# ELU in an attention-plus-feed-forward kernel: minimum on GpSimd, maximum on VectorE from PSUM, no ReLU on ScalarE

## The chip, the cores and the metric

The kernel runs on one core of a Trainium2 chip. The metric is the time of one execution in device microseconds; lower is better. A core has a matrix engine (TensorE, PE in the profile, with its weight loads as PEld), two engines that stream over tiles (VectorE, DVE; ScalarE, ACT), a programmable engine (GpSimd, POOL) and SyncE (SP), which here only issues transfers. TensorE writes its products to PSUM; the other tiles are in SBUF. GpSimd's instructions in this kernel touch SBUF alone.

## The reference

Four batches, eight heads, 768 positions, 64 elements a head. A query sees only the keys whose six sign bits (of a projection) equal its own. The attention's result, as 3072 rows of 512, goes through a feed-forward pair of 512 to 2048 to 512 with an ELU between:

```python
scores = np.where(mask, scale * np.matmul(q, k.transpose(0, 1, 3, 2)), -1e9)
scores = scores - np.max(scores, axis=-1, keepdims=True)
attn = np.exp(scores)
attn = attn / (np.sum(attn, axis=-1, keepdims=True) + 1e-09)
x = np.matmul(attn, v)                      # then (B*S, H*D) = (3072, 512)
h = x @ w_in                                # (3072, 2048)
g = np.where(h > 0.0, h, np.exp(np.minimum(h, 0.0)) - 1.0)
out = g @ w_out                             # (3072, 512)
```

## The kernel before

Products are made in pairs of float16 numbers: each operand is split into a high part (`hi`, the scaled value rounded to float16) and a low part (`lo`, the rest), and three products hi·hi, hi·lo, lo·hi are added up in PSUM. ScalarE makes the high parts (`scaled`, line L143) and VectorE the low parts (`rest`, L152), each with one instruction.

Attention runs in slots of 128 queries of one head against all 768 keys. In a slot TensorE makes the scores (tile `s`, L508, four matrix instructions; there is one `s` buffer, two banks), VectorE copies them to SBUF with a row maximum (`pt`, L520, "the row maximum" below, which also frees `s`), ScalarE makes the exponentials of two slots with their sums (L533, L536, L545), VectorE the reciprocal (L546), ScalarE and VectorE the two halves `hl` (L143, L152), SyncE a transposing transfer into `PT` (L551), and TensorE the product with the values (`av`, L559), which ScalarE and VectorE split into `x` (L568, L569). The loading, scaling and splitting of later queries, keys and values (`qst`, `kst`, `vf`, `nat1q`, `nat2q`, `natk`, `vhl`, `K`, `O`, `zb`) and of the weights (`W`, once) run in between.

The feed-forward part works on chunks of 384 rows: eight chunks, 16 steps each, 128 in all. A step is one call of `first` and later one of `second`. `first(c, f)` makes 128 columns of h for the chunk (12 instructions of 128x384, L588) in one of two `h` banks of PSUM, and then the ELU and the split of it into `g16` (tiles e, hp and g are all parts of one SBUF tensor, `U` in the profile). `second(c, f)` multiplies `g16` with the output weights (nine instructions of 128x512, L624), two steps later, at a chunk's end up to three. At a chunk's end the result `o` is copied out of PSUM and stored by transfers that GpSimd issues (`out_dram`, L638).

The order on TensorE is written out: from the slot at which the feed-forward part begins, its queue follows the program's order, in which steps of `moe_stream` are strewn between the slots of the next chunk's attention by a table of costs. On the other engines the tile framework's scheduler sets the order when the kernel is built: it lists instructions by priority against a timeline of its own, and each engine then works its queue strictly in that order. So an instruction that waits holds up all that stands behind it on its engine.

The ELU of a step is the smaller of exp(h) - 1 and the ReLU of h: exponential (L599) and ReLU (L602) on ScalarE out of the `h` bank, then one instruction on VectorE in SBUF (L603). The `h` bank is free for the step after next once the ReLU has read it.

Of the kernel before, what the change touches and what calls it, by code (L numbers as in the profile page):

```python
# [8 lines left out]
F16 = mybir.dt.float16  # L9
BF16 = mybir.dt.bfloat16  # L10
F32 = mybir.dt.float32
I32 = mybir.dt.int32
AF = mybir.ActivationFunctionType
ALU = mybir.AluOpType
# [52 lines left out]
def lsh_attention_moe(  # L67
# [10 lines left out]
    nc = tc.nc  # L78
# [32 lines left out]

    U = const.tile([P, 3 * 2 * SL], F32, name="U")
    area, at_ = {}, 0
    for name, n, dt in (("e", 2, F32), ("hp", 2, F32), ("g", 4, F16)):
        area[name] = []
        for _ in range(n):
            area[name].append(U[:, at_ : at_ + HALF].bitcast(dt))
            at_ += HALF
# [4 lines left out]
    def part(name):  # L123

        n = taken.get(name, 0)
        taken[name] = n + 1
        return area[name][n % len(area[name])]
# [11 lines left out]
    def scaled(kind, o, x, s):  # L139

        e = engine(kind)
        if e == "A":
            nc.scalar.activation(o, x, AF.Copy, scale=s)  # L143
        elif e == "V":
            nc.vector.tensor_scalar(o, x, s, None, ALU.mult)
        else:
            nc.gpsimd.tensor_scalar(o, x, s, 1.0, ALU.mult, ALU.mult)

    def rest(kind, o, x, s, hi):

        if engine(kind) == "V":
            nc.vector.scalar_tensor_tensor(o, x, s, hi, ALU.mult, ALU.subtract)  # L152
        else:
            nc.gpsimd.tensor_scalar(x, x, s, 1.0, ALU.mult, ALU.mult)
            nc.gpsimd.tensor_tensor(o, x, hi, ALU.subtract)
# [419 lines left out]
    def moe_stream(chunks):  # L575
# [4 lines left out]
        def first(c, f):  # L580
            moe_at[0] = max(moe_at[0], f)
            w = c["nc"] * P
            h = ps_h.tile([P, 512], F32, tag="h", name="h")[:, :w]
            g, fc = f // FG, f % FG
            n = 0
            for t in range(KT):
                for wx, xx in ((0, 0), (0, 1), (1, 0)):
                    nc.tensor.matmul(  # L588
                        h,
                        WH[:, g * KT + t, wx, fc * P : (fc + 1) * P],  # L590
                        c["xs"][t][:, xx, :],
                        start=n == 0,
                        stop=n == 3 * KT - 1,
                    )
                    n += 1
                    if n < 3 * KT:
                        yield w
            e = part("e")[:, :w]
            nc.scalar.activation(e, h, AF.Exp, scale=c["ch"])  # L599

            hp = part("hp")[:, :w]
            nc.scalar.activation(hp, h, AF.Relu, scale=c["ch"])  # L602
            nc.vector.scalar_tensor_tensor(e, e, -1.0, hp, ALU.add, ALU.min)  # L603
            g16 = part("g").rearrange("p (x n) -> p x n", x=2)[:, :, :w]
            scaled("g_hi", g16[:, 0, :], e, c["sg"])
            rest("g_lo", g16[:, 1, :], e, c["sg"], g16[:, 0, :])
            pend.append((c, f, g16))
            yield w
# [32 lines left out]
        for c in chunks:  # L641
            ch = small.tile([P, 1], F32, tag="ch", name="ch", bufs=2)
            sg = small.tile([P, 1], F32, tag="sgg", name="sgg", bufs=2)
            vst = vs[c["b"]][0]
            nc.vector.scalar_tensor_tensor(ch, vst["ex"], 2.0 ** -(V_TOP + W_TOP), wst["ex", 0], ALU.mult, ALU.mult)
            nc.vector.scalar_tensor_tensor(sg, vst["sc"], 2.0**-G_DOWN, wst["sc", 0], ALU.mult, ALU.mult)
            c.update(ch=ch, sg=sg)
            for f in range(NF):
                if f % FG == 0:
                    need_w(f // FG * KT + KT - 1)  # L650
                yield from first(c, f)

                if len(pend) > (3 if pend[0][1] == 0 and c is not chunks[0] else 2):
                    while len(pend) > 2:
                        need_w(NSI + pend[0][1])
                        yield from second(*pend.pop(0))
# [81 lines left out]
    for ns in groups:  # L738
# [3 lines left out]
        for n in ns:  # L742
            at = begin[n] - (PREP0 if early else PREP)[2]

            w = 2 * chunks[pairs[n][0]]["nc"]
# [148 lines left out]
    for G in range(starts[-2] + 1):  # L894
        if G == starts[0]:
            ordered.enter_context(tc.manual_schedule(engines={mybir.EngineType.PE}))
        if G < len(slots):
            n, at = slots[G]
            c = chunks[pairs[n][0]]
# [60 lines left out]
```

## Time and profile before

| | |
|---|---|
| time, median of 3 runs | 952.3 us (950.54 to 952.47) |
| profiled execution, span from first to last instruction | 952.0 us |
| TensorE busy | 817.4 us, 86% |
| ScalarE busy | 741.4 us, 78% |
| VectorE busy | 703.4 us, 74% |
| GpSimd busy | 15.7 us, 2% (24 issues of stores, and memsets at the start) |
| first exponential of the ELU (L599), last | 173.3 us, 938.1 us |

The span of the profiled execution lies within the range of the timed runs, 0.3 us under their median. The shares are means over stages: up to about 170 us weights and the first chunk's attention are prepared, up to about 860 us attention and feed-forward steps run together, and after that the last chunk's feed-forward steps run alone. Idle time of an engine is told as the wait that ended it.

### The profile page before, as it was taken

The page shows a single profiled execution, that of the slowest core. Times are in us where ns is not written, and L with a number is a line of the kernel's source. Part 1 is how long each engine was busy: PE and PEld are TensorE (multiplying, and loading weights), DVE is VectorE, ACT ScalarE, POOL GpSimd, SP SyncE. Part 2 cuts the span into 40 slices and gives each one's busy share as a digit, 9 for nine tenths or more (in the row PEclk, how much of TensorE's full clock was granted, in tenths as well). Part 3 has the DMA queues.
Part 4 walks back from the last instruction along what each step waited for, and adds up shares of the span by engine and source line. Part 5 has one row for each costly group of instructions (what it writes and reads, how often), then busy time and mean ns, then how long its engine had stood idle before and what let it go on. Part 6 is the DMA issues. An engine that isn't in the chain of part 4 may idle for free.

```text
span 952.0 us, 14531 instructions
## 1 busy us (share of the span) xinstructions
PE 817.4 (86%) x4975; PEld 420.6 (44%) x4975; DVE 703.4 (74%) x1524; ACT 741.4 (78%) x1473; POOL 15.7 (2%) x49
## 2 busy tenths in 40 slices
PE   2445555987999999988998999998989999999996
PEld 0112222544545555544554455544445555555553
DVE  6798999887877867678776686787877687764332
ACT  5578876988979878789779787889888788885442
POOL 1000000000000000000000000000000000000000
PEclk9998656999999999999999999999999999999998
DMA  9999898676787768687887758795786767556000
GB/s 284 237 225 217 224 252 170 118 142 145 148 164 166 149 113 140 129 184 120 161 182 135 138 110 148 150 185 102 140 148 130 123 118 150 101 100 100 34 1 35
DMA packets 404587, 138.48 MB, mean 145 GB/s; under 512 B 380960, under 2 KB 398880, under 8 KB 404512
## 3 DMA queue, kind: packets, MB, share of 16 engines
q1 hardware_dynamic: 402432, 131.25, 69.5%
q0 software_dynamic: 1920, 6.29, 1.9%
q8 instruction: 39, 0.64, 0.3%
q14 instruction: 36, 0.29, 0.1%
q10 hardware_dynamic: 160, 0.00, 0.0%
HBM read 35.65 MB, written 6.29 MB: 44 GB/s over the span
## 4 chain that ended last, share of the span: by engine, by line
issue 77%; PE 11%; DMA 5%; DVE 3%; ACT 2%; POOL 1%; POOLq 0%; ACTq 0%; DVEq 0%
PE o L624 3%; PE h L588 3%; PE av L559 2%; PE s L508 2%; DMA K<-natk 1%; DMA O<-nat1q 1%; DMA out_dram<-W 1%; POOL out_dram L638 1%; ACT pt L536 1%; DVE pt L520 1%; DVE hl L152 1%; DMA PT<-hl 1%; DMA vf<-in_v_dram 0%; DVE natk L152 0%; ACT hl L143 0%
## 5 line engine op out<-in xcount | busy, mean ns | idle before, releaser
L624 PE MATMUL o<-W,U 128*128 128x512 f16 x1152 | 280.3, 379 | 4.3 <-ACT W L143 4.2
L588 PE MATMUL h<-x,W 128*128 128x384 f16 x1536 | 280.8, 327 | 0.8 <-ACT x L568 0.6
L588 PEld LDWEIGHTS <-W 128*128 128x128 f16 x1536 | 147.7, 98 | 112.6 <-issue 11.9
L536 ACT ACTIVATE pt<-pt,nb,sg 128x768 f32<-128x768 f32 x192 | 195.3, 1019 | 1.7
L152 DVE SCALAR_TENSOR_TENSOR hl<-pt,r,hl 128x768 f16<-128x768 f32 x192 | 189.5, 1012 | 8.8 <-ACT hl L143 8.4
L143 ACT ACTIVATE hl<-pt,r 128x768 f16<-128x768 f32 x192 | 168.4, 926 | 22.4 <-DVE r L546 22.0
L520 DVE TENSOR_SCALAR_CACHE_REDUCE pt<-s 128x768 f32<-128x768 f32 x177 | 168.1, 949 | 21.8 <-PE s L508 20.7
L508 PE MATMUL s<-K,O 128*128 128x384 f16 x708 | 153.8, 341 | 32.1 <-DVE pt L520 31.7
L624 PEld LDWEIGHTS <-U 128*128 128x128 f16 x1152 | 111.0, 98 | 125.4 <-issue 11.7
L559 PE MATMUL av<-PT,vhl 128*64 128x384 f16 x1152 | 113.8, 347 | 27.1 <-DMA PT<-hl 16.7
L603 DVE SCALAR_TENSOR_TENSOR U<-U 128x384 f32<-128x384 f32 x128 | 71.0, 555 | 86.7 <-ACT U L602 85.7
L508 PEld LDWEIGHTS <-O 128*128 128x128 f16 (+1 forms) x768 | 74.9, 102 | 129.9 <-issue 55.0
L152 DVE SCALAR_TENSOR_TENSOR U<-U,sgg 128x384 f16<-128x384 f32 x128 | 78.4, 612 | 59.7 <-ACT U L143 59.7
L599 ACT ACTIVATE U<-h,ch 128x384 f32<-128x384 f32 x128 | 72.9, 569 | 62.5 <-PE h L588 62.3
L559 PEld LDWEIGHTS <-vhl 128*64 128x64 f16 x1152 | 73.0, 116 | 73.5 <-ACT W L143 13.2
L143 ACT ACTIVATE U<-U,sgg 128x384 f16<-128x384 f32 x128 | 77.8, 608 | 19.9 <-DVE U L603 19.8
L602 ACT ACTIVATE U<-h,ch 128x384 f32<-128x384 f32 x128 | 73.0, 570 | 0.0
L472 PE MATMUL acc<-W,ones 128*128 128x512 bf16 x32 | 17.1, 554 | 33.9 <-DVE W L469 33.9
L536 ACT ACTIVATION_READ_ACCUMULATOR pt<-pt,nb,sg 128x1 f32 x192 | 36.3, 189 | 0.0
L533 ACT ACTIVATE nb<-m,sg 128x2 f32<-128x2 f32 x96 | 27.7, 288 | 8.7 <-DVE pt L520 8.7
L207 ACT ACTIVATE nat1q<-qst 128x384 bf16<-128x384 f32 x30 | 15.5, 517 | 18.9 <-DMA O<-nat1q 18.1
L291 DVE TENSOR_SCALAR zb<-z,pjt 64x384 f16<-64x384 f32 (+1 forms) x48 | 29.1, 606 | 1.2 <-PE z L286 1.2
(102 smaller groups left out, 527.2 us busy)
## 6 DMA issues: line engine op xcount, KB each, us to landing
U<-in_moe_w_in_dram SPq DMA_DIRECT2D x12, 512.0 KB
vf<-in_v_dram SPq DMA_DIRECT2D x16, 384.0 KB
U<-in_moe_w_out_dram SPq DMA_DIRECT2D x12, 512.0 KB
out_dram<-W POOLq DMA_DIRECT2D x24, 256.0 KB, 4.0
qst<-in_q_dram SPq DMA_DIRECT2D x30, 192.0 KB
kst<-in_k_dram SPq DMA_DIRECT2D x14, 384.0 KB
PT<-hl SPq DMA_TRANSPOSE x192
W<-in_moe_w_in_dram SPq DMA_DIRECT2D x4, 512.0 KB
```

What stands on the lines that cost most here:

```text
L143: nc.scalar.activation(o, x, AF.Copy, scale=s)
L152: nc.vector.scalar_tensor_tensor(o, x, s, hi, ALU.mult, ALU.subtract)
L291: nc.vector.tensor_scalar(zb[used], t[used], pj["thr"][used, which : which + 1], (MBIT, -MBIT)[which], ALU.is_gt, ALU.mult)
L508: nc.tensor.matmul(s_tile[:, n, :HALF], st[o][:rows, at, :], kst[kk][:rows, j * NC + n * HC : j * NC + (n + 1) * HC, :].rearrange("p a b - ...
L520: top = nc.vector.tensor_scalar(pt.rearrange("p (n e) -> p n e", n=2), s_tile[:, :, :HALF], CLAMP, None, ALU.max, ALU.max, accum_out=duo[0 ...
L536: nc.scalar.activation(pt, pt, AF.Exp, bias=nb[:, n : n + 1], scale=st["sg"][:, 0:1], accum_out=sm[:, n : n + 1])
L559: nc.tensor.matmul(av[j * D : (j + 1) * D], vt[:, j, c, vx, :], PTs[j][:, :, px, c, :], start=n == 0, stop=n == last,)
L588: nc.tensor.matmul(h, WH[:, g * KT + t, wx, fc * P : (fc + 1) * P], c["xs"][t][:, xx, :], start=n == 0, stop=n == 3 * KT - 1,)
L599: nc.scalar.activation(e, h, AF.Exp, scale=c["ch"])
L602: nc.scalar.activation(hp, h, AF.Relu, scale=c["ch"])
L603: nc.vector.scalar_tensor_tensor(e, e, -1.0, hp, ALU.add, ALU.min)
L624: nc.tensor.matmul(o[t][:, :DO], g16[:, gx, t * P : (t + 1) * P], WH[:, NSI + 1 + f, wx, :], start=f == 0 and i == 0, stop=f == NF - 1 and ...
```

## The change

VectorE's and ScalarE's part of the ELU is written another way: the ELU is the larger of h and min(exp(h) - 1, 0). ScalarE makes the exponential as before. GpSimd takes 1 away and takes the minimum with 0, in place in SBUF (a new instruction, L602 of the changed kernel). VectorE scales h straight out of the PSUM bank and takes the maximum with that (L603, with another form of operands). ScalarE's ReLU and its buffers `hp` go, and `e` has four buffers instead of two, in the same room.

```diff
-    for name, n, dt in (("e", 2, F32), ("hp", 2, F32), ("g", 4, F16)):
+    for name, n, dt in (("e", 4, F32), ("g", 4, F16)):
...
             e = part("e")[:, :w]
             nc.scalar.activation(e, h, AF.Exp, scale=c["ch"])
-            hp = part("hp")[:, :w]
-            nc.scalar.activation(hp, h, AF.Relu, scale=c["ch"])
-            nc.vector.scalar_tensor_tensor(e, e, -1.0, hp, ALU.add, ALU.min)
+            nc.gpsimd.tensor_scalar(e, e, -1.0, 0.0, ALU.add, ALU.min)
+            nc.vector.scalar_tensor_tensor(e, h, c["ch"], e, ALU.mult, ALU.max)
             g16 = part("g").rearrange("p (x n) -> p x n", x=2)[:, :, :w]
             scaled("g_hi", g16[:, 0, :], e, c["sg"])
             rest("g_lo", g16[:, 1, :], e, c["sg"], g16[:, 0, :])
```

TensorE's queue is the same instruction for instruction. The queues of the other engines are set anew by the scheduler from the first step on (before about 170 us they are the same). Three places show how they move. Names carry the number of their buffer; `U_91<-U_91,sgg` is the split of the ELU's result.

VectorE, in the third chunk, before: from one row maximum to the next (the step of h_4128 is the 38th; its VectorE part stands there as `L603`).

```order
L520 TENSOR_SCALAR pt_4115,m_4114<-s_4109 128x768
L152 SCALAR_TENSOR_TENSOR U_91<-U_91,sgg_3751 128x384
L152 SCALAR_TENSOR_TENSOR nat2q_97<-qst_3931,qs_4095,nat1q_96 128x6x64
L162 COPY nat1q_96<-nat1q_96 128x6x64
L152 SCALAR_TENSOR_TENSOR natk_95<-kst_3927,ks_4087,natk_95 128x12x64
L546 RECIPROCAL r_4117<-r_4117 128x2
L603 SCALAR_TENSOR_TENSOR U_91<-U_91 128x384
L520 TENSOR_SCALAR pt_4155,m_4114<-s_4150 128x768
```

After, from the same row maximum on:

```order
L520 TENSOR_SCALAR pt_4115,m_4114<-s_4109 128x768
L152 SCALAR_TENSOR_TENSOR nat2q_97<-qst_3931,qs_4095,nat1q_96 128x6x64
L162 COPY nat1q_96<-nat1q_96 128x6x64
L546 RECIPROCAL r_4117<-r_4117 128x2
L152 SCALAR_TENSOR_TENSOR U_91<-U_91,sgg_3751 128x384
L152 SCALAR_TENSOR_TENSOR natk_95<-kst_3927,ks_4087,natk_95 128x12x64
L520 TENSOR_SCALAR pt_4155,m_4114<-s_4150 128x768
L152 SCALAR_TENSOR_TENSOR hl_4120<-pt_4021,r_4117,hl_4120 128x768
L291 TENSOR_SCALAR zb_4175<-z_4168,pjt_136 64x384
L152 SCALAR_TENSOR_TENSOR hl_4124<-pt_4061,r_4117,hl_4124 128x768
L603 SCALAR_TENSOR_TENSOR U_91<-h_4128,ch_3750,U_91 128x384
L520 TENSOR_SCALAR pt_4195,m_4194<-s_4189 128x768
```

The ELU's VectorE instruction has moved from ahead of the row maximum of s_4150 to behind it and behind two low parts of the attention, right ahead of the next row maximum.

ScalarE at the same place, before:

```order
L599 ACTIVATE U_91<-h_4128,ch_3750 128x384
L602 ACTIVATE U_91<-h_4128,ch_3750 128x384
L143 ACTIVATE hl_4120<-pt_4021,r_4117 128x768
L143 ACTIVATE hl_4124<-pt_4061,r_4117 128x768
L143 ACTIVATE U_91<-U_91,sgg_3751 128x384
L533 ACTIVATE nb_4157<-m_4114,sg_3519 128x2
L143 ACTIVATE nat1q_96<-qst_3933,qs_4095 128x6x64
L536 ACTIVATE pt_4115,sm_4159<-pt_4115,nb_4157,sg_3519 128x768
```

After:

```order
L599 ACTIVATE U_91<-h_4128,ch_3750 128x384
L143 ACTIVATE hl_4120<-pt_4021,r_4117 128x768
L143 ACTIVATE hl_4124<-pt_4061,r_4117 128x768
L533 ACTIVATE nb_4157<-m_4114,sg_3519 128x2
L536 ACTIVATE pt_4115,sm_4159<-pt_4115,nb_4157,sg_3519 128x768
L536 ACTIVATE pt_4155,sm_4159<-pt_4155,nb_4157,sg_3519 128x768
L143 ACTIVATE nat1q_96<-qst_3933,qs_4095 128x6x64
L143 ACTIVATE natk_95<-kst_3929,ks_4087 128x12x64
L545 ACTIVATE r_4197<-sm_4159 128x2
L599 ACTIVATE U_91<-h_4180,ch_3750 128x384
L143 ACTIVATE U_91<-U_91,sgg_3751 128x384
```

The ReLU is gone from between the exponential and the attention's high parts, and the high part of the step's own result has moved behind the next step's exponential.

GpSimd, from the first step on, before:

```order
L638 DMA out_dram<-W 128x512 x24
```

After (the first rows):

```order
L602 ISA
L602 TENSOR_SCALAR U<-U 128x384 x18
L638 DMA out_dram<-W 128x512 x2
L602 TENSOR_SCALAR U<-U 128x384
L638 DMA out_dram<-W 128x512
L602 TENSOR_SCALAR U<-U 128x384 x15
```

The 128 new instructions stand in one queue with the 24 issues of stores, and the third store of a chunk behind the third step of the next.

## Prediction

> **What bounds the kernel now.** I began with the stages, since the change touches nothing ahead of the first ELU at 173.3 us. The view by stretches gives each engine's busy time from there on:
>
> ```profile
> 170.00:250.00 80.00, 69.32 (x433) 35.67 (x432) 67.59 (x139) 73.09 (x147) 0.00 (x0) 0.96 0.69 135
> 250.00:860.00 610.00, 580.39 (x3707) 307.91 (x3706) 460.10 (x977) 507.68 (x1022) 9.89 (x18) 1.00 0.75 141
> 860.00:952.00 92.00, 83.80 (x466) 43.82 (x464) 28.64 (x49) 39.99 (x73) 3.25 (x6) 0.97 0.17 37
> ```
>
> The columns after the length are PE, PEld, DVE, ACT, POOL, the granted clock, the share of the transfers and GB/s. In the long stage TensorE is busy 580.4 of 610 us (95%) at full clock, ScalarE 83%, VectorE 75%. In the short one before it, with the weights still being split, ScalarE is busy 91% and VectorE 84%, and TensorE falls to 87%. TensorE is the bound, and what the change can win or lose is TensorE's waiting. So next the view of waits, for 170 to 860 us (who waits, for whom, us in total, times, longest):
>
> ```profile
> DVE U L603 <- ACT U L602: 48.5, 42, 3.6
> DVE U L152 <- ACT U L143: 45.7, 39, 3.4
> PE s L508 <- DVE pt L520: 24.7, 26, 4.5
> PE av L559 <- DMA PT<-hl: 9.1, 7, 3.2
> PE o L624 <- ACT W L143: 4.2, 4, 2.0
> ```
>
> TensorE waits 24.7 us for row maxima on VectorE (they free the one score buffer), 9.1 us for transposed probabilities and 4.2 us for the copy of a finished output: 38.0 us in 37 waits. None of them is for an ELU or for an `h` bank. After 860 us TensorE waits for nothing until the last stores. 38 us is therefore the ceiling of the gain, 4% of the span.
>
> Then one of the longer waits in the timeline, at the place that the order shows (start, us, engine, instruction, idle time before it):
>
> ```profile
> 410.29 0.60 ACT L143 ACTIVATE U<-U,sgg 128x384 f16<-128x384 f32 x1
> 410.93 0.62 DVE L152 SCALAR_TENSOR_TENSOR U<-U,sgg 128x384 f16<-128x384 f32 x1 [3.39 <-ACT U L143]
> ...
> 412.22 0.56 ACT L599 ACTIVATE U<-h,ch 128x384 f32<-128x384 f32 x1
> 412.26 1.02 DVE L152 SCALAR_TENSOR_TENSOR natk<-kst,ks,natk 128x768 f16<-128x768 f32 x1
> 412.69 0.56 ACT L602 ACTIVATE U<-h,ch 128x384 f32<-128x384 f32 x1
> 413.28 0.56 DVE L603 SCALAR_TENSOR_TENSOR U<-U 128x384 f32<-128x384 f32 x1
> 413.38 1.76 ACT L143 ACTIVATE hl<-pt,r 128x768 f16<-128x768 f32 x2
> 413.76 0.95 DVE L520 TENSOR_SCALAR_CACHE_REDUCE pt<-s 128x768 f32<-128x768 f32 x1
> 414.77 0.81 PE L508 MATMUL s<-K,O 128*128 128x384 f16 x4 [1.71 <-DVE pt L520]
> ```
>
> VectorE stood still 3.39 us for a high part that came late on ScalarE, then worked off what had piled up, and the row maximum at 413.76 came last; TensorE lost 1.71 us. This is the pattern: an in-order queue on VectorE, held up by ScalarE, ahead of a row maximum.
>
> **The change, part by part.** The sum is made against the profiled execution's span of 952.0 us; the median of the runs shown is 952.3, so what is said of one holds for the other within 0.3 us.
>
> *ScalarE loses the ReLU.* The groups by line in 170 to 860 us:
>
> ```profile
> L602 ACT ACTIVATE U<-h,ch 128x384 f32<-128x384 f32 x108 | 61.5, 569 | 0.0
> L603 DVE SCALAR_TENSOR_TENSOR U<-U 128x384 f32<-128x384 f32 x108 | 59.9, 554 | 49.5 <-ACT U L602 48.5
> L569 DVE SCALAR_TENSOR_TENSOR x<-av,x 128x384 f16<-128x384 f32 x28 | 15.4, 550 | 5.4 <-ACT x L568 5.4
> L520 DVE TENSOR_SCALAR_CACHE_REDUCE pt<-s 128x768 f32<-128x768 f32 x161 | 152.8, 949 | 20.8 <-PE s L508 20.7
> ```
>
> 108 of the 128 ReLUs lie in the stage, each takes 0.47 us of ScalarE's queue (412.22 to 412.69 above: one starts before the other has ended). That is 51 us off an engine that is busy 581 of 690 us. All of it lies beside TensorE's work; on the path is only what stands ahead of one of the 37 waits. A step comes every 690/108 = 6.4 us, and the wait above was built up over about as long (VectorE's 3.39 us of standing still and its work after it, 407.5 to 413.8), so about one ReLU stands ahead of each wait: 37 x 0.47 = 17 us. The bounds are 0 (the order puts other ScalarE work, `natk` and `nat1q`, into the freed room, and some waits are VectorE's own) and the ceiling of 38. I take two thirds of the 17, **-11 us**, since most of the waits go back to ScalarE in the end.
>
> *VectorE's instruction changes its operands.* It now reads h from PSUM and e from SBUF. The nearest row is L569, of the same size, which reads PSUM and SBUF: 550 ns against 554 of L603. It costs nothing, 0 us, hidden or not. Its place in the queue is later, behind the low parts of the attention and right ahead of a row maximum. Where the minimum from GpSimd is there by then, this lets the attention's work through earlier, as at 413.28, where 0.48 us stood ahead of the row maximum; where it isn't, the next row maximum waits. I put the two against each other: 0 us, between -3 and the slower cases below.
>
> *GpSimd makes 128 minima.* No row shows such an instruction. The nearest are memsets and the issue of a store after the instruction that released it:
>
> ```profile
> L257 POOL MEMSET W<- 128x384 f16 x2 | 0.8, 420 | 0.0
> L225 POOL MEMSET pjz<- 128x128 f16 x1 | 0.2, 208 | 0.0
> ...
> 943.19 0.69 ACT L143 ACTIVATE W<-o,os 128x512 f32<-128x512 f32 x1 [2.83 <-PE o L624]
> 944.17 0.54 POOL L638 DMA_DIRECT2D out_dram<-W  x1 [54.23 <-ACT W L143]
> ```
>
> Writing 384 float16 elements takes 0.42 us, 0.21 of it for the last 256; the minimum also reads, and moves twice the bytes. Its bounds are 0.42 us and, by doubling that for the bytes and adding a read, some 1.2; I take 0.65, nearer to the memset, as an estimate. The Trainium skill ("GPSIMD Engine Reference", section "Elementwise — side-by-side cycle accounting") has 1.8 cycles an element at 1.2 GHz as its best general case, from which I estimate 0.58 us; the sum would be the same. GpSimd starts 0.29 us after ScalarE's end (943.19 + 0.69 to 944.17), so the result is there 0.94 us after the exponential, 0.45 later than the ReLU was (about 0.5 after it). As work it hides fully: 108 x 0.65 = 70 us on an engine that is idle.
>
> *VectorE and GpSimd together.* No row shows GpSimd reading SBUF beside VectorE. If they don't disturb each other the cost is 0; if VectorE stands for the full length of each minimum it is 108 x 0.65 = 70 us of VectorE. How much of VectorE's delay reaches TensorE: 26 of the 161 row maxima were waited for, 16%. So the bounds are 0 and 11 us. In between lies a clash only where both read at once, by VectorE's instructions with two SBUF sources:
>
> ```profile
> L152 DVE SCALAR_TENSOR_TENSOR hl<-pt,r,hl 128x768 f16<-128x768 f32 x162 | 159.7, 1012 | 7.5 <-ACT hl L143 7.2
> L152 DVE SCALAR_TENSOR_TENSOR U<-U,sgg 128x384 f16<-128x384 f32 x108 | 66.0, 612 | 45.7 <-ACT U L143 45.7
> L152 DVE SCALAR_TENSOR_TENSOR nat2q<-qst,qs,nat1q 128x384 f16<-128x384 f32 x24 | 14.6, 609 | 3.6 <-ACT nat1q L143 3.5
> L152 DVE SCALAR_TENSOR_TENSOR vhl<-vf,vs,vhl 128x384 f16<-128x384 f32 x24 | 13.8, 613 | 0.0
> L152 DVE SCALAR_TENSOR_TENSOR natk<-kst,ks,natk 128x768 f16<-128x768 f32 x12 | 12.1, 1012 | 0.6 <-ACT natk L143 0.5
> L152 DVE SCALAR_TENSOR_TENSOR W<-W,w1s 128x512 f16<-128x512 f32 x16 | 11.9, 745 | 0.4 <-ACT W L143 0.2
> ```
>
> They are 278 us of 690 (40%), 346 instructions, one start in 2 us. A minimum of 0.65 us meets such a start with 0.65/2 = 0.33 and holds it half its length, 0.11 us; where it has itself stood behind one (0.4) and another follows (0.4), the whole 0.65, 0.10 us. 0.21 x 108 = 23 us of VectorE, 16% of it on the path: **+4 us**, which I take, in the lower half because the two meet by chance.
>
> *The `h` bank is let go later.* Before, ScalarE's ReLU was its last reader; now VectorE is. The timeline of the last chunk shows the room that the steps alone leave, and that of the 18th step the narrow place at a chunk's start, where two steps follow each other:
>
> ```profile
> 895.73 0.57 ACT L602 ACTIVATE U<-h,ch 128x384 f32<-128x384 f32 x1
> 900.82 2.11 PE L588 MATMUL h<-x,W 128*128 128x384 f16 x12
> ...
> 287.31 0.56 ACT L602 ACTIVATE U<-h,ch 128x384 f32<-128x384 f32 x1
> ...
> 287.90 0.56 DVE L603 SCALAR_TENSOR_TENSOR U<-U 128x384 f32<-128x384 f32 x1
> ...
> 289.04 1.46 PE L588 MATMUL h<-x,W 128*128 128x384 f16 x8
> ```
>
> In the last chunk the bank is free at 896.30 and used again at 900.82: 4.5 us, of which the change takes about one. At the narrow place the last four of the eight start the 20th step in this bank at about 289.7 (four of 0.16 us after 289.04). ScalarE had it free at 287.87; VectorE would have at 288.46, and 0.45 later with GpSimd's chain: 0.8 us are left, less whatever stands ahead on VectorE. At six such boundaries I take a third of a us each, **+2 us**; bounds 0 and 6 x 1.5 = 9. In the last chunk, which ends the span, nothing: 0.
>
> *The first steps.* The one wait for an ELU is in 170 to 250 us, where ScalarE is fullest:
>
> ```profile
> PEld L624 <- DVE U L152: 0.4, 1, 0.4
> ```
>
> That chain has no room and grows: **+1 us**, bounds 0 and 4. The stores behind minima on GpSimd: a minimum of 0.65 us ahead of a transfer that a chunk has 100 us for, 0.
>
> Sum: -11 + 0 + 4 + 2 + 1 = -4, **948.0 us**.
>
> **Rivals.**
> 1. *Much of the ceiling comes back.* For it: 94 us of VectorE's idle time in the stage are waits for ScalarE on ELU tiles, and the waits pile up. Against: TensorE pays only 38. With 25 of them gone and 5 lost elsewhere, 932 us.
> 2. *No difference.* For it: the freed ScalarE slots are filled at once by other splits, row maxima still come when VectorE gets to them, and its work is the same. With a third of the 17 us gained and the same losses, 952 - 6 + 7 = 953 us.
> 3. *GpSimd and VectorE shut each other out* (slower). The low parts with two SBUF sources stand right ahead of the ELU's instruction in the new order, so a minimum that has to wait for one leaves VectorE idle next. With a minimum of about 1 us that costs VectorE its whole length each time: 108 us, 16% of it 17 us, against the net gain of 8 without contention: 961 us. It decides from 8/0.16/108 = 0.46 us of VectorE lost per minimum on. Against it: no row, and VectorE has 162 us of room in the stage. The Trainium skill ("SBUF — State Buffer", section "Who interferes with whom") states just such a lock: a VectorE instruction with two SBUF inputs and a GpSimd instruction that reads SBUF exclude each other for the whole instruction. By that rule the 4 us above would be the least, and no trace here shows it yet.
> 4. *The ELU's chain comes late* (slower). If the minimum takes 2 us, six chunk boundaries lose about 1.5 us each at the `h` bank, and the first steps 5: 952 - 11 + 4 + 14 = 959 us. Against it: the 4.5 us of room elsewhere.
>
> **How the numbers follow.** A difference within 0.2% (1.9 us) can't be told from none here. Chances: the forecast 0.40 (its own range 943 to 950), rival 1 0.08, rival 2 0.20, rival 3 0.20, rival 4 0.12. Faster 0.48, same 0.20, slower 0.32. The range takes in most of the slower cases, whose size hangs on an unseen duration, and part of rival 1: 937 to 963 us.
>
> **What would show it.** Right: ScalarE busy about 128 x 0.47 = 60 us less, L603 at about 0.55 us, TensorE's waits for row maxima under 20 us in the stage, none for `h` over 3 us. Wrong: low parts (L152) with a mean clearly over 1.01 us (rival 3), L603 waiting for GpSimd in long stretches just ahead of row maxima, minima of over 1 us, or waits of L588 for L603 (rival 4).

## The result and the profile after

The changed kernel takes 936.3 us (median of four runs, 934.7 to 939.2) against 952.4 for the kernel before on the same chip: 0.983 of it, 95% interval 0.980 to 0.986. The forecast of 948.0 had the sign right and a quarter of the size, and its range ended 0.7 us above the result.

The page's first part, of the changed kernel: busy time, share of the span and instructions of each engine.

```profile
span 934.0 us, 14523 instructions
PE 816.6 (87%) x4975; PEld 419.9 (45%) x4975; DVE 717.6 (77%) x1524; ACT 690.7 (74%) x1345; POOL 229.1 (25%) x177
```

TensorE's work is as it was (817.4 us before), ScalarE has lost 51 us, GpSimd gained 213. The span of this execution is 18.0 us shorter (the medians differ by 16.0). The same stretches as before (columns PE, PEld, DVE, ACT, POOL, granted clock, transfers, GB/s; the last is cut at the new end):

```profile
170.00:250.00 80.00, 72.60 (x454) 37.46 (x452) 70.39 (x143) 69.84 (x137) 21.31 (x12) 0.96 0.72 137
250.00:860.00 610.00, 594.64 (x3805) 314.73 (x3804) 479.31 (x988) 479.10 (x942) 178.01 (x118) 0.99 0.76 143
860.00:934.00 74.00, 66.12 (x353) 34.24 (x351) 21.19 (x34) 21.89 (x36) 27.25 (x22) 0.98 0.06 22
```

In the long stage TensorE is busy 97% instead of 95%. Summed up from the trace, its gaps of over 50 ns after 170 us went from 40.3 to 22.7 us, 17.6 of the 18.0; ahead of 170 us they are the same (79.1 and 79.5). The waits in 170 to 860 us (who, for whom, us in total, times, longest):

```profile
DVE U L603 <- POOL U L602: 48.1, 42, 1.9
DVE U L152 <- ACT U L143: 20.0, 26, 2.5
PE s L508 <- DVE pt L520: 15.3, 13, 3.3
PE h L588 <- DVE U L603: 3.3, 2, 2.2
PE av L559 <- DMA PT<-hl: 1.2, 3, 0.7
PE o L624 <- DVE U L152: 0.9, 1, 0.9
```

TensorE's waits for row maxima fell from 24.7 to 15.3 us, those for transposed probabilities from 9.1 to 1.2. New are waits for an `h` bank, 3.3 us, and for a low part of the ELU's result, 0.9 us. VectorE waits as long at the ELU's instruction as before (48.1 against 48.5 us), only now for GpSimd. The groups of that stage (count, busy us, mean ns, idle time before them and its cause):

```profile
L602 POOL TENSOR_SCALAR U<-U 128x384 f32<-128x384 f32 x112 | 189.0, 1687 | 630.6 <-ACT U L599 629.9 <-ACT r L545 0.6
L603 DVE SCALAR_TENSOR_TENSOR U<-h,ch,U 128x384 f32<-128x384 f32 x112 | 68.5, 612 | 48.1 <-POOL U L602 48.1
L152 DVE SCALAR_TENSOR_TENSOR hl<-pt,r,hl 128x768 f16<-128x768 f32 x165 | 164.7, 1020 | 18.9 <-ACT hl L143 18.7
L162 DVE COPY nat1q<-nat1q 128x384 f16<-128x384 f16 x24 | 7.9, 327 | 0.0
```

A minimum takes 1.69 us on the mean there, far above the 0.65 that was assumed, and the ELU's instruction 0.61 instead of 0.55. The line's own view (ns at the least, at the median and at the most, first and last start):

```profile
L602 POOL TENSOR_SCALAR U<-U x128: 1484/1494/3849, 174.7 to 920.9; 128x384 f32<-128x384 f32 x128
```

By the prediction's own signs (minima of over 1 us, VectorE waiting for them) this kernel should have been slow, and it isn't. The timeline of the place that the prediction showed, the same row maxima (start, us, engine, instruction):

```profile
406.56 0.56 ACT L599 ACTIVATE U<-h,ch 128x384 f32<-128x384 f32 x1
...
407.20 1.86 POOL L602 TENSOR_SCALAR U<-U 128x384 f32<-128x384 f32 x1 [4.58 <-ACT U L599]
407.62 0.95 DVE L520 TENSOR_SCALAR_CACHE_REDUCE pt<-s 128x768 f32<-128x768 f32 x1
...
408.50 1.01 DVE L152 SCALAR_TENSOR_TENSOR hl<-pt,r,hl 128x768 f16<-128x768 f32 x1
...
409.43 0.60 DVE L291 TENSOR_SCALAR zb<-z,pjt 64x384 f16<-64x384 f32 x1
...
409.96 1.00 DVE L152 SCALAR_TENSOR_TENSOR hl<-pt,r,hl 128x768 f16<-128x768 f32 x1
...
410.89 0.60 DVE L603 SCALAR_TENSOR_TENSOR U<-h,ch,U 128x384 f32<-128x384 f32 x1
```

The minimum is done at 409.06. By then VectorE is in the work that the new queue put ahead of the ELU (a row maximum, two low parts, `zb`), and takes up the ELU at 410.89 without a wait. The row maximum that stood at 413.76 before, behind 3.39 us of standing still, is the one at 407.62 here. The whole kernel is ahead by then (the step's exponential is at 406.56 instead of 412.22), so this place alone didn't give the difference of 6 us.

The 3.39 us had a root that the prediction's cut didn't show. ScalarE, before:

```profile
407.43 0.84 ACT L207 ACTIVATE natk<-vf 128x768 bf16<-128x768 f32 x1 [2.09 <-DMA vf<-in_v_dram]
...
410.29 0.60 ACT L143 ACTIVATE U<-U,sgg 128x384 f16<-128x384 f32 x1
```

And after:

```profile
403.80 0.83 ACT L207 ACTIVATE natk<-vf 128x768 bf16<-128x768 f32 x1
...
405.23 0.60 ACT L143 ACTIVATE U<-U,sgg 128x384 f16<-128x384 f32 x1
```

Before, ScalarE stood still 2.09 us for a transfer of `vf`, ahead of two attention exponentials and of the high part that VectorE waited for; an estimate from these rows is that VectorE would have waited some 1.3 us without it. In the new order those exponentials come first, and the instruction that reads `vf` waits for nothing.

### The profile page after: what moved, and what is told of

Its sections match the earlier page's. It is cut to its first block, busy times and chain, and to the rows that moved or that the text cites. A ratio compares the mean times of both kernels' runs of the same rounds, so it can differ in the third digit from the quotient of the medians.

```text
span 934.0 us, 14523 instructions
## 1 busy us (share of the span) xinstructions
PE 816.6 (87%) x4975; PEld 419.9 (45%) x4975; DVE 717.6 (77%) x1524; ACT 690.7 (74%) x1345; POOL 229.1 (25%) x177
## 4 chain that ended last, share of the span: by engine, by line
PE 49%; DVE 19%; DMA 14%; ACT 8%; issue 7%; POOL 2%; SPq 1%; ACTq 0%; POOLq 0%; DVEq 0%
PE o L624 17%; PE h L588 17%; PE s L508 7%; PE av L559 6%; DVE pt L520 4%; DMA K<-natk 4%; DVE hl L152 4%; ACT pt L536 3%; POOL U L602 2%; DMA O<-nat1q 2%; ACT hl L143 2%; DMA W<-in_moe_w_out_dram 2%; DMA out_dram<-W 1%; DVE vhl L152 1%; PE z L286 1%
## 5 line engine op out<-in xcount | busy, mean ns | idle before, releaser
L602 POOL TENSOR_SCALAR U<-U 128x384 f32<-128x384 f32 x128 | 212.9, 1663 | 670.4 <-ACT U L599 669.8
L152 DVE SCALAR_TENSOR_TENSOR hl<-pt,r,hl 128x768 f16<-128x768 f32 x192 | 191.5, 1019 | 20.0 <-ACT hl L143 19.9
L603 DVE SCALAR_TENSOR_TENSOR U<-h,ch,U 128x384 f32<-128x384 f32 x128 | 78.4, 612 | 79.8 <-POOL U L602 79.8
L599 ACT ACTIVATE U<-h,ch 128x384 f32<-128x384 f32 x128 | 73.0, 570 | 59.1 <-PE h L588 58.6
L152 DVE SCALAR_TENSOR_TENSOR U<-U,sgg 128x384 f16<-128x384 f32 x128 | 79.1, 619 | 30.9 <-ACT U L143 30.9
L286 PEld LDWEIGHTS <-pjz 128*32 128x32 f16 (+1 forms) x320 | 9.3, 94 | 43.9 <-issue 29.8
```

What stands on the lines that cost most here:

```text
L602: nc.gpsimd.tensor_scalar(e, e, -1.0, 0.0, ALU.add, ALU.min)
L603: nc.vector.scalar_tensor_tensor(e, h, c["ch"], e, ALU.mult, ALU.max)
```

## The experiments

Times are medians, ratios are against the kernel before on the same chip with their 95% intervals. "Gaps" are TensorE's after 170 us, summed as above.

**Taking the change apart.** First the ReLU alone: the kernel before without it; VectorE reads the exponential twice (the positive part of the ELU is left out), nothing on GpSimd.

```diff
-            hp = part("hp")[:, :w]
-            nc.scalar.activation(hp, h, AF.Relu, scale=c["ch"])
-            nc.vector.scalar_tensor_tensor(e, e, -1.0, hp, ALU.add, ALU.min)
+            nc.vector.scalar_tensor_tensor(e, e, -1.0, e, ALU.add, ALU.min)
```

> The kernel before, with ScalarE's ReLU left out and nothing else moved to another engine: VectorE's instruction stays in SBUF with two sources, but its second source is the exponential itself, so this kernel computes exp(h) - 1 in place of the ELU. GpSimd does nothing in the steps. Theory 1 (the gain is ScalarE's time: 128 ReLUs of 0.47 us that stand in its queue ahead of the attention's work): 930 to 938 us, the whole gain of the change or a little more, and TensorE's waits between 170 and 860 us fall from 40 to about 20 us. Theory 2 (the gain comes from what VectorE and GpSimd do differently, the instruction out of PSUM and the later place of it): 946 to 953 us. Theory 3 (the scheduler's new order is luckier by chance): anything, with no relation to ScalarE's load.

942.7 us, 0.989 (0.983 to 0.995): 10 us. Then the changed kernel with the ReLU back on ScalarE, its result unread, and two buffers each of `e` and `hp` (that line is left out here):

```diff
+            hp = part("hp")[:, :w]
+            nc.scalar.activation(hp, h, AF.Relu, scale=c["ch"])
             nc.gpsimd.tensor_scalar(e, e, -1.0, 0.0, ALU.add, ALU.min)
```

> The changed kernel, with ScalarE's ReLU put back behind the exponential; its result is written to hp and read by nobody. So ScalarE has its old load, and GpSimd and VectorE have the new one; e and hp have two buffers each, as before the change. Theory 1 (ScalarE's time): the gain goes, 948 to 956 us, ScalarE busy about 740 us. Theory 2 (VectorE and GpSimd): 934 to 940 us. Theory 4 (four buffers of e instead of two): 948 to 953 us as well, which the run with two buffers alone tells apart.

947.2 us, 0.992 (0.989 to 0.995). That is 11 us more than its fair partner, the changed kernel with two `e` buffers (936.2, below). By both, the ReLU seemed worth 10 to 11 us, which was the prediction's term, and 6 us were left over that nothing in the sum gave. Next the minimum on VectorE, and the buffers alone:

```diff
-            nc.gpsimd.tensor_scalar(e, e, -1.0, 0.0, ALU.add, ALU.min)
+            nc.vector.tensor_scalar(e, e, -1.0, 0.0, ALU.add, ALU.min)
```

> The changed kernel with the minimum on VectorE instead of GpSimd, in place in SBUF. VectorE has 128 instructions more; a copy of 128x384 in SBUF took it 0.25 us (16 bit), a shift of 128x512 in 32 bit 0.42 us, so some 0.33 us each, 42 us in all. Theory 1 (ScalarE's time): most of the gain stays, 934 to 944 us: VectorE goes from 77% to about 81% busy. Theory 2 (taking work to GpSimd is the gain): 948 us or more.

```diff
-    for name, n, dt in (("e", 4, F32), ("g", 4, F16)):
+    for name, n, dt in (("e", 2, F32), ("hp", 2, F32), ("g", 4, F16)):
```

> The changed kernel with two buffers of e, as before the change, the other two buffers unused. Theories 1, 2: 934 to 939 us, as the changed kernel; a buffer is needed again 12 us later and the chain of a step takes about 5. Theory 4 (the buffers carry the gain): 945 to 953 us.

935.1 us, 0.981 (0.977 to 0.984), and 936.2, 0.981 (0.978 to 0.985). The gain needs neither GpSimd nor the buffers. Two theories for the 6 us were left: A, the order of the queues, B, the operands of VectorE's instruction. Two kernels make a square with the former ones: `f1` without the minimum (VectorE takes the maximum of h and exp(h) itself), `f2` with the minimum but with VectorE's old operands.

```diff
 f1, against the changed kernel
-            nc.gpsimd.tensor_scalar(e, e, -1.0, 0.0, ALU.add, ALU.min)
 f2, against the changed kernel
-            nc.vector.scalar_tensor_tensor(e, h, c["ch"], e, ALU.mult, ALU.max)
+            nc.vector.scalar_tensor_tensor(e, e, -1.0, e, ALU.add, ALU.min)
```

> The changed kernel without GpSimd's minimum: VectorE takes the maximum of h out of PSUM and exp(h) itself (1 is not subtracted and the minimum with 0 left out). VectorE's and ScalarE's queues are set in 95% as in the kernel without the ReLU (942.7 us there), where the VectorE instruction reads SBUF only; only the form of that instruction differs, and the h bank is let go by VectorE instead of ScalarE. Theory A (the 6 us beyond the ReLU come from the queue order that the longer chain through GpSimd leads the scheduler to, with the ELU's work behind the attention's): 942 to 944 us, as without the ReLU. Theory B (they come from VectorE's form, PSUM in place of two SBUF sources): 935 to 938 us.

> The other corner of the square: GpSimd's minimum as in the changed kernel, but VectorE's instruction reads it from SBUF alone, with the operands that it had before, and h is not read (the positive part of the ELU is left out). The h bank is let go by ScalarE's exponential. ScalarE's queue is in 97% that of the changed kernel. Theory A (queue order): 935 to 938 us, as the changed kernel or 1 to 2 us under it, since no wait of TensorE for an h bank is left. Theory B (form of VectorE's instruction): 941 to 944 us, as the kernel that only lacks the ReLU. Contention (the rival of two SBUF sources against GpSimd) would show here as VectorE's instruction at over 0.7 us and a time over 938.

936.8 us, 0.984 (0.982 to 0.986), and 932.8, 0.979 (0.977 to 0.981). Neither theory held: `f1` came out as B had it, `f2` came nearer to A, a little under its range. What `f1` shows besides is the price of the operands:

```profile
L603 DVE SCALAR_TENSOR_TENSOR U<-h,ch,U 128x384 f32<-128x384 f32 x111 | 67.7, 610 | 22.2 <-ACT U L599 22.2
```

0.61 us without any GpSimd beside it, so the 0.06 us by which L603 grew belong to the form of the instruction, not to contention. The kernel before with its ReLU moved to VectorE was to tell more:

```diff
-            nc.scalar.activation(hp, h, AF.Relu, scale=c["ch"])
+            nc.vector.tensor_scalar(hp, h, c["ch"], 0.0, ALU.mult, ALU.max)
```

> The kernel before with the ReLU made by VectorE out of PSUM instead of ScalarE; no GpSimd. The ELU's last instruction stands about 0.5 us of VectorE's work later than before, the attention's low parts 0.5 us earlier, and VectorE has 128 instructions (some 60 us) more. Theory A (ScalarE's relief of 10 us and an order that lets the attention through earlier): 934 to 938 us, as with both instructions on VectorE reading h last (935.1). Theory B (PSUM form of the last instruction): 940 to 944, as that instruction reads SBUF only here. If VectorE's load counted: 945 or more.

948.0 us, 0.995 (0.993 to 0.996). This is the third case: it fits that 128 instructions of 0.61 us more on VectorE eat most of the gain. But this kernel has an order of its own too, and the minimum on VectorE, of 0.35 us, had not shown such a cost, so it isn't shown.

**Contention.** A second minimum on GpSimd behind each, on a spare part of the same tensor (two `e` buffers, and a first clearing of the spare part, are left out here):

```diff
             nc.gpsimd.tensor_scalar(e, e, -1.0, 0.0, ALU.add, ALU.min)
+            nc.gpsimd.tensor_scalar(area["hp"][0], area["hp"][0], -1.0, 0.0, ALU.add, ALU.min)
```

> The changed kernel with a second GpSimd minimum of the same size behind each (on a spare part of the same SBUF tensor, read by nobody); e has two buffers, which alone gave 936.2 us. GpSimd is then busy about 390 us in the long stages instead of 190. If GpSimd and VectorE exclude each other at VectorE's cost, VectorE's low parts with two SBUF sources grow by as much again as they did (1012 to 1020 ns, so some 1030 ns) or more and the time rises by over 3 us. If it is GpSimd that stands back, VectorE stays within 1% and the time at 935 to 939 us, while the minima grow from 1.69 us mean; a part of the rise could then also come from the ELU's own minimum waiting behind the spare one.

945.9 us, 0.991 (0.989 to 0.994), 9.6 more than the changed kernel with two `e` buffers. The scheduler let the spare minima run ahead, all between 162 and 528 us, so GpSimd was busy 301 of 358 us there. The groups in 170 to 528 us (L602 is the spare minimum in this kernel):

```profile
L602 POOL TENSOR_SCALAR U<-U 128x384 f32<-128x384 f32 x124 | 206.5, 1666 | 5.6
L152 DVE SCALAR_TENSOR_TENSOR hl<-pt,r,hl 128x768 f16<-128x768 f32 x81 | 84.9, 1074 | 6.5 <-ACT hl L143 6.2
L162 DVE COPY nat1q<-nat1q 128x384 f16<-128x384 f16 x14 | 4.9, 351 | 0.0
```

With GpSimd at 84% the low parts take 1.07 us instead of 1.01 and the copy 0.35 instead of 0.25. Contention is there and grows with GpSimd's load. VectorE's busy time in the stretch is only 3 us more (295 against 292 in the changed kernel with two `e` buffers), but for 597 instructions instead of 610; by the means of the groups, its low parts and copies took about 9 us longer than there (an estimate). How much of the 9.6 us is this, and how much the other order of this kernel, stays open.

**The order by itself.** The scheduler gives every variant a new order, so all of the runs above mix two things. The next ones don't: VectorE's, ScalarE's and SyncE's queues of one kernel were put exactly into the order of another, by a chain of edges that only order (no instruction, no semaphore). The traces show VectorE's and ScalarE's instructions in exactly that order, and TensorE's and GpSimd's as they were (the edit is shortened):

```diff
         lsh_attention_moe(tc, *args)
+        # _o: the engine's instructions in the other kernel's order
+        for _a, _b in zip(_o, _o[1:]):
+            tc.add_manual_dep(_b, _a.name, mybir.DependencyInfo(mybir.DependencyClass.NoSync, ...
```

> The changed kernel with the instructions of VectorE, ScalarE and SyncE held in the order that they have in the kernel before (the ReLU's places taken out), by ordering edges that cost no instruction. The work is that of the changed kernel, only the queues are the old ones. Theory A (ScalarE's relief gives 10 us and the scheduler's new order the other 6): 941 to 944 us. Theory C (the relief gives all 16, the order nothing): 935 to 938 us. Theory D (an order fits the kernel that it was made for, and here GpSimd's longer chain stands in a queue that expects a short one): 945 us or more, with VectorE's waits for the minimum far above 48 us and TensorE's for an h bank above 5 us.

> The kernel before, ReLU and all, with the three queues in the order of the changed kernel, each ReLU right behind its exponential on ScalarE. Theory A: 945 to 948 us, the order's 6 us without the relief. Theory C: 951 to 954 us, no change. Theory D: 955 us or more, as ScalarE's queue with the ReLUs in it comes late for an order that was made without them.

> The kernel before without its ReLU (VectorE's instruction reads the exponential twice; the positive part of the ELU is left out; nothing on GpSimd), in the old order exactly. This is ScalarE's relief alone: no new order, no GpSimd, no PSUM operand. In an order of its own it took 942.7 us. Theory A: 941 to 944 us. Theory C: 935 to 938 us. If part of the gain of 10 there was already its own new order: 945 to 949 us.

> The same kernel without the ReLU (positive part of the ELU left out, nothing on GpSimd) in the order of the changed kernel. Theory A: 934 to 937 us, as the changed kernel, whose order this is. Theory C: also 935 to 938 us, but then with the same time in the old order. If the changed kernel lost time to GpSimd's chain or its contention, this shows it: 930 to 934 us, since VectorE doesn't wait for a minimum here.

| instructions | old order | the changed kernel's order |
|---|---|---|
| the kernel before, with the ReLU | 953.8 us | 939.8 us, 0.985 (0.982 to 0.987) |
| without the ReLU, nothing on GpSimd | 946.4 us, 0.992 (0.990 to 0.995) | 936.4 us, 0.981 (0.978 to 0.984) |
| the changed kernel | 974.6 us, 1.021 (1.019 to 1.024) | 936.3 us, 0.983 (0.980 to 0.986) |

The corners that are a kernel in its own order have no edges, and no kernel was run with edges in its own order. The 936.3 is the run of the result, where the kernel before took 952.4.

This settles where most of the gain is: in the order. The kernel before gains 14.1 us by the order alone, with every ReLU in its place; none of the theories had so much. Theory A was right that the order counts, C fell, and D was right for the changed kernel in the old order only (its waits for an `h` bank, which D expected there as well, didn't come). Taking out the ReLU is worth 7.4 us in the old order and 3.4 in the new, less than the 10 to 11 read off the first pairs. GpSimd's minimum with the new operands costs nothing that the intervals show in the new order and 28.2 us in the old one. The waits of the kernel before in the changed kernel's order:

```profile
DVE U L152 <- ACT U L143: 29.0, 39, 3.1
DVE hl L152 <- ACT hl L143: 20.8, 27, 2.7
PE s L508 <- DVE pt L520: 14.9, 17, 3.0
DVE U L603 <- ACT U L602: 8.9, 14, 1.9
```

VectorE's standing still for ELU tiles (L603 and L152 of `U`) fell from 94.2 us to 37.9 with the same instructions, and TensorE's waits for row maxima to where the changed kernel has them. The changed kernel in the old order, its waits and the place of the timeline again:

```profile
DVE U L603 <- POOL U L602: 108.7, 88, 4.7
ACT U L143 <- DVE U L603: 48.7, 56, 3.0
PE s L508 <- DVE pt L520: 41.2, 38, 5.0
```

```profile
416.32 1.76 POOL L602 TENSOR_SCALAR U<-U 128x384 f32<-128x384 f32 x1 [6.96 <-ACT U L599]
...
418.12 0.62 DVE L603 SCALAR_TENSOR_TENSOR U<-h,ch,U 128x384 f32<-128x384 f32 x1 [1.31 <-POOL U L602]
418.65 0.94 DVE L520 TENSOR_SCALAR_CACHE_REDUCE pt<-s 128x768 f32<-128x768 f32 x1
...
419.66 0.80 PE L508 MATMUL s<-K,O 128*128 128x384 f16 x2 [3.21 <-DVE pt L520]
```

Here the minimum ends at 418.08, VectorE stands still for it, the row maximum comes behind, and TensorE waits 3.21 us. The ELU's chain comes late here, as in rival 4, at a price of 28 us, but it is paid at the row maxima (41.2 us of TensorE's waits, against 18.0 without the minimum in this order); the waits for an `h` bank, by which that rival was priced, didn't come. The new order is what keeps the changed kernel from this.

**Which part of the order.** Five variants of the kernel before with its ReLU, and one with the minimum on VectorE in the changed kernel's order. `h1` and `h2` hold back one kind of instruction by 128 edges each and leave the rest to the scheduler; `i2` has 142 edges; `h3`, `h4` and `i1` take over a whole order as above.

```diff
+        # h1: row maximum or low part ahead of it in the changed order > VectorE's ELU instruction (L603)
+        # h2: exponential ahead of it in the changed order > ScalarE's high part of the ELU's result
+        # i2: attention's low part > what stands right behind it in the changed order, on VectorE
+        tc.add_manual_dep(_b, _a.name, mybir.DependencyInfo(mybir.DependencyClass.NoSync, ...
```

> The kernel before, ReLU and all, with one thing added: each of VectorE's 128 ELU instructions (L603) is held behind the row maximum or low part behind which it stands in the changed kernel's order; the scheduler sets the rest anew. The ELU then stands 1.2 us of VectorE's work later than before, as in the changed kernel, the attention's low parts 0.15 us earlier (0.37 there). If VectorE's standing still for the ELU (94 us in the long stages) is what delays the row maxima: 939 to 943 us, with VectorE's waits at L603 under 20 us. If ScalarE's queue is what counts, or the low parts' place: 948 to 953 us.

956.0 us, 1.002 (0.999 to 1.004): no gain, though the wait at L603 went as expected:

```profile
DVE U L152 <- ACT U L143: 55.7, 45, 3.9
PE s L508 <- DVE pt L520: 20.9, 16, 3.9
DVE U L603 <- ACT U L602: 12.0, 13, 2.0
```

Part of the wait has moved on to the low part of the ELU's result (55.7 us against 45.7 before). The two together are 67.7 us, 26 less than before, and this is worth nothing; the changed kernel has as much of it (48.1 + 20.0). So how long VectorE stands still in all doesn't give the time; what stands behind it then must count as well.

> The kernel before, with the high part of each step's ELU result on ScalarE held behind the exponential behind which it stands in the changed kernel's order; nothing else is held. VectorE's ELU instruction stays where it was (0.04 us later). If VectorE's place is what counts: 950 to 954 us, no change. If ScalarE's waiting for VectorE's result (10 us) or its order counts: 941 to 947 us.

948.7 us, 0.994 (0.992 to 0.996): 5 us less than the kernel before, between the two cases, a little nearer to that of no change, with the waits at L603 nearly as they were (43.8 us).

> The changed kernel with the minimum on VectorE (0.35 us each, 128 more instructions there, right ahead of the maximum) instead of GpSimd, and all three queues held in the changed kernel's order. In an order of its own this kernel took 935.1 us. If GpSimd's 1.5 us minimum costs the changed kernel nothing in its order: 935 to 938 us. If its late arrival (VectorE waits 48 us for minima) costs some of the gain: 931 to 934 us. If 45 us more work on VectorE ahead of the row maxima counts: 938 to 942 us.

940.4 us, 0.986 (0.984 to 0.989), against 0.983 (0.980 to 0.986) of the changed kernel: in this order the minimum seems better on GpSimd, by 3 to 4 us.

> The kernel before, ReLU and all, in the order of the kernel with GpSimd's minimum and VectorE's instruction in SBUF (932.8 us). ScalarE's queue is in 97% that of the changed kernel. Order alone: 935 to 940 us, as the kernel before in the changed kernel's order (939.8) less up to 4 us, since that order took 3.5 us less with its own kernel. If that kernel owed its time to the missing ReLU and the early release of the h bank instead: 940 to 944 us.

938.1 us, 0.983 (0.981 to 0.986). The arithmetic before, given this order, is within 2 us of the changed kernel.

> The kernel before, ReLU and all, in the order of the kernel without GpSimd's minimum (f1, 936.8 us). In it VectorE's ELU instruction stands 0.14 us of work later than before (1.14 in the changed kernel's order), the attention's low parts 0.34 us earlier (0.37 there). If the low parts' earlier place is what the order brings: 939 to 943 us, the f1 time and 3 to 7 us for the ReLU. If the ELU's later place is needed: 947 to 953 us.

945.6 us, 0.992 (0.990 to 0.994): 7.5 us, half of what the changed kernel's order gives and between the two cases.

> The kernel before, ReLU and all, with 142 ordering edges on VectorE alone: what stands right behind an attention low part in the changed kernel's order must stay behind it; the scheduler sets the rest anew. The low parts then stand 0.43 us of work earlier than before, the ELU's instruction 0.44 later. If the low parts' place counts: 939 to 944 us. If the gain needs the whole order, ScalarE's queue with it: 946 to 953 us.

969.1 us, 1.017 (1.014 to 1.020). The low parts first, forced by edges on VectorE alone, lose 16 us, which neither case had. Not all of it is waiting: in the profiled execution, the fastest of the six (a span of 961.6 us against 952.0), TensorE's gaps are 5 us more and its busy time 6 us more, for the same instructions.

No single piece that was tried gives more than half of the 14 us. But the scheduler moved far more than the pieces that were held: counted from the traces, 85% of VectorE's and 90% of ScalarE's instructions keep the old sequence in `h1`, 84% and 89% in `i2`, and no more than 81% and 85% in the changed kernel. So `h1` and `i2` show that the ELU's later place on VectorE, or that of the low parts, isn't enough, and not that it has no part in the gain. The 14 us come with the whole order, ScalarE's and SyncE's queues included. VectorE's queue alone, or ScalarE's alone, was not exchanged, and which pieces together do it is left open.

A lead is in the traces. ScalarE's waits for transfers in 170 to 860 us, such as the one for `vf` above, summed up for the kernels with the arithmetic unchanged:

| kernel | ScalarE's waits for transfers | time |
|---|---|---|
| `i2` | 42.0 us | 969.1 us |
| the kernel before | 39.7 us | 953.8 us |
| `h1` | 38.8 us | 956.0 us |
| `h2` | 33.7 us | 948.7 us |
| `i1` | 29.7 us | 945.6 us |
| the changed kernel's order (`g2`) | 21.9 us | 939.8 us |
| `h4` | 21.2 us | 938.1 us |

The kernels that gain are those in which these waits fell, and the further they fell the more. That holds only with the ReLU on ScalarE (without it, in the old order, there are 49.7 us of them at 946.4), and no run changed them by themselves, so it isn't shown that they are the cause.

No run with the whole ELU in it is faster than the changed kernel by more than the intervals: the minimum on VectorE in its own order (935.1) is level with it.

## Why the prediction was wrong, by its steps

- **The place in the queue: 0 us, measured -14 for the order.** This is the step that failed. The prediction counted the new order as the ELU's later place on VectorE alone, called it a gain where the minimum is there in time and a loss where not, and set the two to 0, with -3 as the best. That bound rested on no row but one 0.48 us instruction ahead of one row maximum. The place to look was already quoted: VectorE stands still for 94 us on ELU tiles, once for 3.39 us ahead of a late row maximum. The prediction put this down to ScalarE's load; with that load unchanged the order alone takes 56 of the 94 us away, and at the place quoted a wait of 2.09 us for a transfer, which the new order avoids, made the high part late. Where only the ELU's place was held and the scheduler set the rest (`h1`), nothing was gained. What the prediction had no term for is the order of all the rest, ScalarE's queue included.
- **ScalarE's relief: -11 us, measured -3.4 in the new order, -7.4 in the old.** The right sign, too much by a factor of 1.5 to 3. The term took it that about one ReLU stands ahead of each wait and that its time is passed on. Without the ReLU, in the old order, ScalarE waits 49.7 us for transfers in the stage instead of 39.7, and 56.9 for TensorE instead of 33.9: much of the freed time is spent in its own waits. It is busy 51 us less in the changed kernel, not 60. The pairs `e1` and `e2`/`e4`, which gave 10 and 11, had changed order too.
- **The minimum: 0.65 us estimated, 1.49 measured** (the median of the 128; the mean is 1.66). It is above the upper bound of 1.2, which came from a memset. The Trainium skill ("GPSIMD Engine Reference", section "Elementwise — side-by-side cycle accounting") gave an estimate of 0.58 us by its best case; the trace has 2.6 times that.
- **Its cover.** "As work it hides fully" was right for the span, but not for the reason given (an idle engine): at the place shown the minimum is done 1.9 us after the exponential, VectorE waits 48 us for minima in the stage, and they hide because the new queue has work ahead of their consumer; in the old one they cost 28 us, the new operands included.
- **VectorE's operands: 0 us by L569.** 0.61 us, not 0.55, some 6 us of VectorE in the stage. Together with the minimum it costs nothing that shows in the new order (936.4 without the two, 936.3 with them); no run prices it alone in one order.
- **Contention: +4 us, 0.21 us of VectorE per minimum.** Measured: the low parts went from 1012 to 1020 ns, those of `U` from 612 to 619, the copy from 251 to 327: together about 4 us for 112 minima, 0.04 us each, against the 0.46 from which rival 3 would have decided. The Trainium skill ("SBUF — State Buffer", section "Who interferes with whom") states the lock; the trace agrees that the two hold each other up, but not for a whole instruction. At 227.71 us a minimum of 1.49 us and a low part of 1.01 us that starts 0.47 us into it run side by side, and neither is longer than alone. GpSimd bears more of it: 37 of its minima take over 1.6 us, up to 3.85, all of them beside a low part or a copy, 21 us above the median in all.
- **The `h` bank: +2, and the first steps: +1.** 3.3 us of waits for the bank in the stage, 1.1 among the first steps and 2.2 behind the 50th exponential, the same place of a chunk as the 18th, and 0.9 us for a low part. The mechanism was right and the size nearly so, though one boundary pays instead of six a little each. In the last chunk TensorE waits for nothing, as forecast.
- **16% of VectorE's delay reaches TensorE.** In the old order the minimum put 78 us more of waiting on VectorE (30.8 to 108.7 us at L603) and 28.2 on the time, 24 of them in TensorE's gaps: about a third, with the new operands' share in it. The 16% is a share of the row maxima that are waited for, and it understated here what a delay ahead of them does.
- **The rivals.** Rival 1 said that much of the ceiling comes back, 932 us, at a chance of 0.08: the nearest to what happened, with a cause that nobody named. Rival 4 (the late chain) is real in the old order, 28 us, paid at the row maxima and not at the `h` bank as it was priced, and the new order prevents it. Rival 3's cost stayed at 0.04 us a minimum.

The sum with the measured terms: -14.1 for the order, -3.4 for the ReLU, 0 for GpSimd, its contention and the bank together (936.4 without them, 936.3 with them), 953.8 to 936.3; the last comes from another comparison, by whose ratio of 0.983 it would be 937.5.

## What to carry to other kernels

Where a scheduler sets the queues, a change of one instruction is two changes, the work and the order, and the second can be the larger: hold the order fixed by ordering edges and price the two apart before believing either. A wait named after an instruction (VectorE for ScalarE's ReLU) needn't be cured by making that instruction cheaper; ask first what held up the engine that is waited for (here a transfer, in part), and whether the waiting instruction could stand behind other work. The slow minimum on an idle engine was free here only where the queue of its consumer had work to put ahead of it: about 0 us in one order, 28 in the other.

## What the runs showed of the hardware that was not expected

- GpSimd's two-operation instruction with constants on 128x384 float32 in place takes 1.49 us at the median (1.48 at the least); VectorE does the same in 0.35 us (39.2 us for 112 in the kernel with the minimum there).
- A VectorE instruction of scalar and two tensors takes 0.61 us with one tensor from PSUM and float32 written, 0.55 with both from SBUF; the one from PSUM that writes float16 (L569) takes 0.55.
- A copy of 384 float16 elements on VectorE goes from 0.25 to 0.33 us on the mean beside the minima and to 0.35 with GpSimd busy 84% of the time: six of the 24 start 0.1 us behind a minimum and take 0.56, the rest are as before. The row maximum, which reads PSUM, stays at 0.95 throughout.
